# Linear attention plus routed MLP on one core: one-pass norm, K weights by row blocks, another warm-up, tile 3 transposed by DMA

## The chip, the cores and the metric

The kernel runs on one core of one Trainium2 chip. The metric is device time in microseconds (us) of one execution. TensorE (PE in the profile, PEld for its weight loads) does the matmuls and some transposes, VectorE (DVE) and ScalarE (ACT) the elementwise work, GpSimd (POOL) small work on columns and masks, SyncE (SP) issues most of the transfers. Each engine works through its own queue in order; semaphores tie the queues together.

## The reference

```python
def _layernorm(x, axis=-1, eps=1e-5):
    m = jnp.mean(x, axis=axis, keepdims=True)
    v = jnp.var(x, axis=axis, keepdims=True)
    return (x - m) / jnp.sqrt(v + eps)

def _A_ref(x, wqkv, wo):                     # H = 32 heads of 20
    q, k, v = split_heads(x @ wqkv)
    phi = lambda t: jnp.where(t > 0, t + 1, jnp.exp(t)) + 1e-6
    pq, pk = phi(q), phi(k)
    kv = jnp.einsum("bhsd,bhse->bhde", pk, v)
    z = jnp.einsum("bhsd->bhd", pk)
    num = jnp.einsum("bhqd,bhde->bhqe", pq, kv)
    den = jnp.einsum("bhqd,bhd->bhq", pq, z)[..., None] + 1e-6
    return merge_heads(num / den) @ wo

def _B_ref(x, w_r, w_gate, w_up, w_down):    # the C = 8 rows with the largest x @ w_r
    r = x @ w_r
    idx = jnp.argsort(-r, axis=-1)[:, :C]
    y = (_silu(x_sel @ w_gate) * (x_sel @ w_up)) @ w_down * _sigmoid(r_sel)
    return x + scatter_add(zero, idx, y)

xn = _layernorm(x)                           # x: (1, 2048, 640), bf16
return x + _A_ref(xn, A_wqkv, A_wo) + _B_ref(xn, B_w_r, B_w_gate, B_w_up, B_w_down)
```

Both branches read the same normalised rows. Everything is bf16 in memory; the intermediate size of the routed MLP is 1536.

## The kernel before, in words

The 2048 rows are 16 tiles of 128 rows (`T`), the 640 columns are 5 blocks of 128 (`KC`). `XX[:, t, 1, :]` holds tile t of x, `XX[:, t, 0, :]` the normalised tile, `xnT` the normalised rows transposed.

Every instruction is written out by hand in the order in which its engine takes it (`manual_schedule`), so that the order of the statements is the order of each engine's queue.

The kernel has a first pass over the 16 tiles and then work on weights, queries and outputs.

For each tile the first pass does the following.

- *Norm.* `ln_a` and `ln_b` (L159, L162) take the statistics of each half of the columns on DVE, `ln_g` (L165) joins them to mean and variance in `MV`, which are bf16 values kept in the upper halves of f32 words. `ln_s` (L198, L199) adds eps on DVE and raises to the power 0.5 on POOL. `ln_c` (L204 on ACT, L206 on DVE) writes mean minus x to a buffer `c`. `ln_xn` (L211, L213) takes the reciprocal of the root and multiplies `c` by it into `XX[:, t, 0, :]`. Tiles 1 and 5 get their statistics from ACT (`ln_act`, L173 to L177) and their root from POOL (`ln_msq`, `ln_var`, L186 to L193).
- *Transposing.* Tiles 0 to 3 are transposed by PE (`tr_pe`, L220) in five blocks, and copied out of PSUM by ACT in two pieces (L224). Tiles 4 to 15 are transposed by a DMA from SP (`tr_dma`, L229).
- *K.* `K(t)` (L251) multiplies the transposed tile by the K weights, in two halves of 320 columns; the second half has one more column, the router's weights `w_r`. `PHe` and `PHr` (L267, L270) take exp and relu on ACT, `PHb` (L286) joins them on DVE to `pk`.
- *G.* `G(t)` (L291, L296) adds the tile's product of normalised rows and `pk` to PSUM, where it stays until tile 15. `ones(t)` (L302, POOL) sets one column of the normalised tile to 1 first.

From tile 4 on a loop runs `K(t)`, then on DVE `PHb(t - 1)` and the norm of tiles up to t + 4, then `G(t - 1)`. The tiles before that are written out one by one (L380 to L454), and that is the part that the change reorders. There PE's order is K(2), tile 3's transposes, G(0), K(3), G(1), G(2), K(4).

The start, ahead of that: SP issues the loads of x tiles 0 to 2, the first half of the K weights, x tile 3, the second half in five pieces, and the other tiles. The router's column gets into the K weights by a transpose on PE (L138) and a copy on ACT (L141). PE does matmuls on zeros ahead of and behind that transpose: `warm4` (L122, f32, 512 columns) and `warm` (L127, bf16). A DMA transposes a block of zeros into the last columns of `xnT` (L379), which are written again later.

Behind the first pass PE goes on with the queries (L502), the small products of `G` with the V and output weights, the routed MLP, and the output tiles (L755), which DVE adds to x (L768) and SP stores.

Of the kernel before, what the change touches and what calls it, by code (L numbers as in the profile page):

```python
# [38 lines left out]
def kernel(  # L39
# [27 lines left out]
    def st(shape, dt, name, tag=None):  # L67
# [6 lines left out]
    wk = st([P, KC * (D + 1)], BF16, "wk", "wkM")  # L74
# [14 lines left out]
    halfc = st([P, 1], BF16, "halfc")  # L89
    epsb = st([P, 1], BF16, "epsb")  # L90
# [8 lines left out]
    wkh = [wk[:, 0 : KC * HW].rearrange("p (k c) -> p k c", k=KC),  # L99
           wk[:, KC * HW : KC * (D + 1)].rearrange("p (k c) -> p k c", k=KC)]  # L100
# [11 lines left out]
    ld(sp, XX[:, 1, 1, :], x_v[:, 1, :])  # L112
    ld(sp, XX[:, 2, 1, :], x_v[:, 2, :])
    ld(sp, wkh[0], wqkv_v[:, :, D : D + HW])
    ld(sp, XX[:, 3, 1, :], x_v[:, 3, :])


    zero32 = zero[:].bitcast(F32)

    def warm4(n):  # L120
        for _ in range(n):
            pe.matmul(PS[:, 7, :], lhsT=zero32[:, 0:P],  # L122
                      rhs=zero32[:, 0:256].unsqueeze(1).to_broadcast([P, 2, 256]), start=True, stop=True)

    def warm(n, w=512):
        for _ in range(n):
            pe.matmul(PS[:, 7, 0:w], lhsT=zero[:, 0:P], rhs=zero[:, 0:w], start=True, stop=True)  # L127
# [9 lines left out]
    warm4(1)  # L137
    pe.transpose(PS[:, 3, :].bitcast(BF16)[:, 0:KC], wr[:], ident[0:KC, 0:KC])  # L138
    warm4(1)
    warm(1)  # L140
    act.copy(wkh[1][:, :, HW], PS[:, 3, :].bitcast(BF16)[:, 0:KC])  # L141
    for kc in range(KC):
        ld(sp, wkh[1][:, kc, 0:HW], wqkv_v[:, kc, D + HW : 2 * D])
# [43 lines left out]

    def ln_var(t):
        pool.tensor_tensor(out=MV[:, t, 1:2], in0=sm[:, t, 1:2], in1=msq[:, 0:1], op=ALU.subtract)
        t2 = tmp.tile([P, 1], BF16, tag="t2", name="t2", bufs=4)  # L190
# [4 lines left out]
    def ln_s(t):
        t2 = tmp.tile([P, 1], BF16, tag="t2", name="t2", bufs=4)
        ss[t] = tmp.tile([P, 1], BF16, tag="s", name="s", bufs=4)
        dve.tensor_scalar(out=t2[:], in0=MV[:, t, 1:2], scalar1=EPS_BF16, scalar2=None, op0=ALU.add)  # L198
        pool.tensor_tensor(out=ss[t][:], in0=t2[:], in1=halfc[:], op=ALU.pow)  # L199

    def ln_c(t, eng):
        cs[t] = tmp.tile([P, D], BF16, tag="c", name="c", bufs=3)
        if eng is act:
            act.activation(cs[t][:], XX[:, t, 1, :], AF.Identity, bias=MVf[:, t, 0:1], scale=-1.0)  # L204
        else:
            dve.tensor_scalar(out=cs[t][:], in0=XX[:, t, 1, :], scalar1=MVf[:, t, 0:1], scalar2=-1.0,  # L206
                              op0=ALU.subtract, op1=ALU.mult)

    def ln_xn(t, parts=((0, D),)):
        c = cs[t]  # L210
        dve.reciprocal(SR[:, t : t + 1], ss[t][:])  # L211
        for a, b in parts:
            dve.tensor_scalar(out=XX[:, t, 0, a:b], in0=c[:, a:b], scalar1=SR[:, t : t + 1], scalar2=-1.0,  # L213
                              op0=ALU.mult, op1=ALU.mult)
# [32 lines left out]
    def K(t, hs=(0, 1), b=6):  # L247
        for h in hs:
            w = HW + h
            for kc in range(KC):  # L250
                pe.matmul(  # L251
                    PS[:, b + h, off(t, h) : off(t, h) + w],
                    lhsT=xnT[:, kc, t * P : (t + 1) * P],
                    rhs=wkh[h][:, kc, 0:w],
                    start=(kc == 0),
                    stop=(kc == KC - 1),
                )
# [121 lines left out]
    sp.dma_start_transpose(xnT[:, 0:4, S - P : S], zero[:])  # L379
# [567 lines left out]
```

## Time and profile before

| | us |
|---|---|
| median of 3 runs (range) | 108.45 (108.4 to 109.05) |
| the profiled execution, its own time | 108.45 |
| its span, first to last instruction | 106.7 |
| PE busy | 101.7 (95%) |
| DVE busy | 84.3 (79%) |
| ACT busy | 74.8 (70%) |
| POOL busy | 27.8 (26%) |

The span is what the profile shows; 1.75 us of the execution lie around it. A line of the profile begins with the start in us and the duration in us, or, in the tables of groups, ends with the busy time in us and the mean of one instruction in ns. L numbers are lines of the kernel before. Matmuls are pipelined: a row's duration holds the way through the array, so that the next one starts before it ends.

### The profile page before, as it was taken

To read this page: it belongs to the slowest core of one execution; us is meant where nothing else is said; L and a number is where in the kernel's file an instruction comes from. 1 tells how busy PE (TensorE), PEld (TensorE's weight loads), DVE (VectorE), ACT (ScalarE), POOL (GpSimd) and SP (SyncE) were. 2 spreads that over 40 slices of the span, in tenths; PEclk is the share of its full clock that TensorE was granted. 3 is DMA by queue.
4 is the path that set the end of the run, shared out by engine and by line. 5 is a ranking of instruction groups with operands and counts; after the bars stand their busy time and mean duration, and the time that the engine had idled before them with its cause. 6 is when DMAs were issued, how large, how long until landed. Compare 5 with 4: busy or idle time off the path is not lost.

```text
span 106.7 us, 2600 instructions
## 1 busy us (share of the span) xinstructions
PE 101.7 (95%) x923; PEld 62.6 (59%) x923; DVE 84.3 (79%) x207; ACT 74.8 (70%) x163; POOL 27.8 (26%) x79
## 2 busy tenths in 40 slices
PE   5979999999999999999999999999999999999990
PEld 1245656666666666667556545655656677777760
DVE  1789997999998999974898996729598696888870
ACT  4649996888877777888497999997688499200000
POOL 7437235456222222000000593500006200000410
PEclk9999999999999999999999999999999999999999
DMA  2999961435566875889998999901560224796344
GB/s 75 272 276 336 339 82 38 81 74 77 112 141 135 118 138 123 175 219 381 234 399 274 352 339 386 311 26 31 170 237 0 63 95 126 177 364 227 123 126 123
DMA packets 23247, 19.68 MB, mean 184 GB/s; under 512 B 10818, under 2 KB 21698, under 8 KB 23234
## 3 DMA queue, kind: packets, MB, share of 16 engines
q1 hardware_dynamic: 22712, 19.45, 65.5%
q8 instruction: 7, 0.11, 0.4%
q0 software_dynamic: 288, 0.01, 0.4%
q10 hardware_dynamic: 234, 0.06, 0.2%
q14 instruction: 6, 0.05, 0.2%
HBM read 13.80 MB, written 3.65 MB: 164 GB/s over the span
## 4 chain that ended last, share of the span: by engine, by line
PE 84%; DVE 7%; POOL 2%; issue 2%; ACT 1%; DVEq 0%; POOLq 0%
PE PS L502 21%; PE PS L755 19%; PE PS L251 15%; PE PS L291 15%; PE PS L296 3%; PE PS L122 2%; PE PS L678 2%; PE PS L715 2%; DVE XX L213 1%; DVE pk L286 1%; POOL s L199 1%; DVE stats L162 1%; PE PS L566 1%; PE PS L737 1%; PE PS L310 1%
## 5 line engine op out<-in xcount | busy, mean ns | idle before, releaser
L251 PE MATMUL PS<-wk,xnT 128*128 128x320 bf16 (+1 forms) x160 | 24.7, 300 | 0.6 <-ACT xnT L224 0.4
L291 PE MATMUL PS<-pk,XX 128*128 128x512 bf16 x80 | 23.2, 378 | 0.1
L502 PE MATMUL PS<-xnT,wq 128*128 128x512 bf16 x100 | 23.0, 380 | 0.0
L755 PE MATMUL PS<-Mb,pqT 128*128 128x320 bf16 (+2 forms) x165 | 22.1, 295 | 0.0
L251 PEld LDWEIGHTS <-xnT 128*128 128x128 bf16 x160 | 15.4, 98 | 7.4 <-ACT xnT L224 0.9
L755 PEld LDWEIGHTS <-pqT 128*128 128x128 bf16 x165 | 15.8, 97 | 6.4 <-issue 0.2
L267 ACT ACTIVATE ek<-PS 128x320 bf16<-128x320 f32 x32 | 14.3, 446 | 5.2 <-PE PS L251 5.2
L502 PEld LDWEIGHTS <-wq 128*128 128x128 bf16 x100 | 11.3, 118 | 9.0
L557 DVE SCALAR_TENSOR_TENSOR pqT<-qe,qr 128x512 bf16<-128x512 bf16 x20 | 13.5, 683 | 2.0 <-ACT qr L509 1.7
L768 DVE TENSOR_TENSOR o<-PS,XX 128x640 bf16<-128x640 f32 x15 | 12.2, 820 | 3.6 <-PE PS L755 2.8
L508 ACT ACTIVATE qe<-PS 128x512 bf16<-128x512 f32 x20 | 12.2, 609 | 3.8 <-PE PS L502 3.3
L270 ACT ACTIVATE rk<-PS 128x320 bf16<-128x320 f32 x32 | 14.4, 449 | 0.0
L199 POOL TENSOR_TENSOR s<-t,halfc 128x1 bf16<-128x1 bf16 x14 | 8.6, 617 | 21.7 <-DVE t L198 21.7
L296 PE MATMUL PS<-pk,XX 128*128 128x128 bf16 x64 | 14.0, 219 | 0.0
L286 DVE SCALAR_TENSOR_TENSOR pk<-ek,rk 128x640 bf16<-128x640 bf16 x16 | 13.0, 815 | 0.9 <-ACT rk L270 0.7
L291 PEld LDWEIGHTS <-XX 128*128 128x128 bf16 x80 | 7.7, 98 | 8.1
L509 ACT ACTIVATE qr<-PS 128x512 bf16<-128x512 f32 x20 | 12.1, 607 | 0.0
L204 ACT ACTIVATE c<-XX,MVf 128x640 bf16<-128x640 bf16 x10 | 8.4, 839 | 1.7 <-DVE MVf L165 1.6
L241 ACT ACTIVATE XX<-XX,MR,SR 128x640 bf16<-128x640 bf16 x11 | 9.4, 914 | 0.0
L159 DVE BATCH_NORM_STATS2 stats<-XX 128x6 f32<-128x320 bf16 x14 | 6.8, 486 | 1.9 <-DMA XX<-in_A_x_dram 1.9
L213 DVE TENSOR_SCALAR XX<-c,SR 128x640 bf16<-128x640 bf16 (+2 forms) x17 | 6.3, 377 | 1.3
L296 PEld LDWEIGHTS <-XX 128*128 128x128 bf16 x64 | 6.2, 97 | 1.3 <-issue 0.4
(125 smaller groups left out, 104.7 us busy)
## 6 DMA issues: line engine op xcount, KB each, us to landing
out_dram<-o SPq DMA_DIRECT2D x15, 160.0 KB, 2.3
wg<-in_B_w_gate_dram SPq DMA_DIRECT2D x5, 384.0 KB, 8.3
wu<-in_B_w_up_dram SPq DMA_DIRECT2D x5, 384.0 KB, 5.9
wd<-in_B_w_down_dram SPq DMA_DIRECT2D x1, 1920.0 KB, 10.7
XX<-in_A_x_dram SPq DMA_DIRECT2D x2, 640.0 KB, 7.1
wv<-in_A_wqkv_dram SPq DMA_DIRECT2D x5, 160.0 KB, 2.9
wq<-in_A_wqkv_dram SPq DMA_DIRECT2D x1, 800.0 KB, 5.4
hi_d<-XX SPq DMA_DIRECT2D x1, 800.0 KB, 4.5
```

What stands on the lines that cost most here:

```text
L251: pe.matmul(PS[:, b + h, off(t, h) : off(t, h) + w], lhsT=xnT[:, kc, t * P : (t + 1) * P], rhs=wkh[h][:, kc, 0:w], start=(kc == 0), stop=( ...
L267: act.activation(phis[t][0][:, h * HW : (h + 1) * HW], phi_src(t, h, b), AF.Exp)
L270: act.activation(phis[t][1][:, h * HW : (h + 1) * HW], phi_src(t, h, b), AF.Relu)
L286: dve.scalar_tensor_tensor(out=pk[:, t, :], in0=ek[:], scalar=1.0, in1=rk[:], op0=ALU.min, op1=ALU.add)
L291: pe.matmul(PS[:, a, :], lhsT=lhsT, rhs=pk[:, t, 0:512], start=(t == 0), stop=(t == T - 1),)
L296: pe.matmul(PS[:, 5, a * P : (a + 1) * P], lhsT=lhsT, rhs=pk[:, t, 512:D], start=(t == 0 and a == 0), stop=(t == T - 1), skip_group_check= ...
L502: pe.matmul(PS[:, bank, :], lhsT=by5(wq[:, kc, :])[:, m, :], rhs=xnT[:, kc, tb * TBLK : (tb + 1) * TBLK], start=(kc == 0), stop=(kc == KC ...
L508: act.activation(e, PS[:, bank, :], AF.Exp)
L509: act.activation(r, PS[:, bank, :], AF.Relu)
L557: dve.scalar_tensor_tensor(out=pqT[:, m, tb * TBLK : (tb + 1) * TBLK], in0=e, scalar=1.0, in1=r, op0=ALU.min, op1=ALU.add,)
L755: pe.matmul(PS[:, b_, 0 : c1 - c0], lhsT=pqT[:, kc, t * P : (t + 1) * P], rhs=Mb[:, kc, c0:c1], start=(kc == 0), stop=(kc == KC - 1))
L768: dve.tensor_tensor(out=ot[:].rearrange("p (h c) -> p h c", h=2), in0=PS[:, b : b + 2, 0:HW], in1=XX[:, t, 1, :].rearrange("p (h c) -> p h ...
```

## The change

- **Norm in one pass.** `ln_s`, `ln_c` and the variants for tiles 1 and 5 go. `ln_r` has ACT take Ln of variance plus eps and then Exp of -0.5 times that, which is the reciprocal root, into `SR`. `ln_xn` reads x and does (x - mean) * `SR` in one DVE instruction. The statistics of tiles 1 and 5 are taken on DVE like the others. The bf16 roundings between the steps fall away.
- **K weights in row blocks.** `wk` becomes one tile of five row blocks with a pitch of 656 columns (`WS`), loaded by five DMAs of 128 rows by 640 columns right behind x tile 1. The buffer `Mb`, which takes its place later, gets the same pitch.
- **Loads.** x tiles 2 to 11 follow the K weights; tiles 12 to 15 and the copies of the mask `bm2` are issued in the loop, at tile 5. The DMA that transposes zeros follows tiles 8 to 11.
- **Warm-up from constants.** `warm4` multiplies a constant that the program's preamble sets, instead of the memset tile. Three calls stand ahead of the router's transpose, one behind it; `warm` goes.
- **First tiles reordered.** K(0) goes block by block through both halves, tile 1's transposes stand between its fourth and fifth block, tile 2's between the third and fourth block of K(1)'s second half; the second PSUM copies of tiles 1 and 2 go to DVE. ACT's queue begins with the router's copy, Ln and Exp of tile 0, the first copy of tile 0, Ln and Exp of tile 1, the second copy of tile 0.
- **Tile 3** is transposed by DMA; PE's order is then K(2), G(0), K(3), G(1), G(2), K(4).

```diff
-    wk = st([P, KC * (D + 1)], BF16, "wk", "wkM")
+    wk = st([P, KC, WS], BF16, "wk", "wkM")
...
     ld(sp, XX[:, 1, 1, :], x_v[:, 1, :])
+    for kc in range(KC):
+        ld(sp, wk[:, kc, 0:D], wqkv_v[:, kc, D : 2 * D])
     ld(sp, XX[:, 2, 1, :], x_v[:, 2, :])
-    ld(sp, wkh[0], wqkv_v[:, :, D : D + HW])
     ld(sp, XX[:, 3, 1, :], x_v[:, 3, :])
+    ld(sp, XX[:, 4:6, 1, :], x_v[:, 4:6, :])
+    ld(sp, XX[:, 6:8, 1, :], x_v[:, 6:8, :])
+    ld(sp, XX[:, 8:12, 1, :], x_v[:, 8:12, :])
+    sp.dma_start_transpose(xnT[:, 0:4, S - P : S], zero[:])
...
-            pe.matmul(PS[:, 7, :], lhsT=zero32[:, 0:P],
-                      rhs=zero32[:, 0:256].unsqueeze(1).to_broadcast([P, 2, 256]), start=True, stop=True)
+            pe.matmul(PS[:, 7, :], lhsT=nc.const_aps.tensor(0.0, (P, P), F32),
+                      rhs=nc.const_aps.tensor(0.0, (P, 512), F32), start=True, stop=True)
...
-    warm4(1)
+    warm4(3)
     pe.transpose(PS[:, 3, :].bitcast(BF16)[:, 0:KC], wr[:], ident[0:KC, 0:KC])
     warm4(1)
-    warm(1)
-    act.copy(wkh[1][:, :, HW], PS[:, 3, :].bitcast(BF16)[:, 0:KC])
-    for kc in range(KC):
-        ld(sp, wkh[1][:, kc, 0:HW], wqkv_v[:, kc, D + HW : 2 * D])
+    act.copy(wk[:, :, D], PS[:, 3, :].bitcast(BF16)[:, 0:KC])
...
+    def ln_r(t):
+        act.activation(lnv[:, t : t + 1], MV[:, t, 1:2], AF.Ln, bias=eps5[:])
+        act.activation(SR[:, t : t + 1], lnv[:, t : t + 1], AF.Exp, scale=-0.5)
...
     def ln_xn(t, parts=((0, D),)):
-        c = cs[t]
-        dve.reciprocal(SR[:, t : t + 1], ss[t][:])
         for a, b in parts:
-            dve.tensor_scalar(out=XX[:, t, 0, a:b], in0=c[:, a:b], scalar1=SR[:, t : t + 1], scalar2=-1.0,
-                              op0=ALU.mult, op1=ALU.mult)
+            dve.tensor_scalar(out=XX[:, t, 0, a:b], in0=XX[:, t, 1, a:b], scalar1=MVf[:, t, 0:1],
+                              scalar2=SR[:, t : t + 1], op0=ALU.subtract, op1=ALU.mult)
...
+    consts_e()
     ln_a(0)
     ln_b(0)
     ln_g(0)
-    ln_s(0)
-    ln_msq(1)
-    ln_c(0, dve)
-    ln_c(1, dve)
+    ln_r(0)
+    ln_a(1)
     ln_xn(0, ((0, 3 * P), (3 * P, D)))
-    tr_pe(0, 0, act, act)
-    ln_var(1)
-    ln_a(2)
+    tr_pe(0, 0, act, act, (0,))
+    ln_b(1)
+    ln_g(1)
+    ln_r(1)
+    tr_pe(0, 0, act, act, (1,))
+    ones(0)
     ln_xn(1)
-    ln_b(2)
+    for kc in range(KC):
+        for h in range(2):
+            K_mm(0, h, kc, 6)
+        if kc == 3:
+            ln_a(2)
+            ln_b(2)
+            tr_pe(1, 2, act, dve)
+            ones(1)
     ln_g(2)
...
+    ln_xn(3)
+    tr_dma(3)
+    ones(3)
+    K(2)
     PHb(0)
...
```

163 lines of the change are left out of this document (47 added, 116 removed).

## The prediction

> **What bounds the kernel now.** The page first, for the span and the engines.
>
> ```profile
> span 106.7 us, 2600 instructions
> PE 101.7 (95%) x923; PEld 62.6 (59%) x923; DVE 84.3 (79%) x207; ACT 74.8 (70%) x163; POOL 27.8 (26%) x79
> GB/s 75 272 276 336 339 82 38 81 74 77 112 141 135 118 138 123 175 219 381 234 399 274 352 339 386 311 26 31 170 237 0 63 95 126 177 364 227 123 126 123
> ```
>
> TensorE (PE) is busy for 95% of the span, which is only an average. The stretches of 6 us say where it is not (columns: stretch, its length, then PE, PEld, DVE, ACT, POOL busy, clock, DMA share, GB/s).
>
> ```profile
> 14.00:20.00 6.00, 5.85 (x43) 3.48 (x42) 5.19 (x14) 5.09 (x15) 2.59 (x7) 1.00 0.35 67
> 20.00:26.00 6.00, 6.00 (x45) 3.73 (x44) 5.58 (x18) 4.94 (x12) 3.17 (x11) 1.00 0.37 57
> 92.00:98.00 6.00, 6.00 (x46) 4.29 (x45) 5.62 (x8) 0.00 (x0) 0.00 (x0) 1.00 0.88 296
> ```
>
> All 13 stretches from 20 to 98 us have PE busy 6.00 of 6.00. So the kernel has two parts: a start of some 15 us in which engines wait for each other, and then a stream of matmuls without a gap. The chain that ended last shows the seam.
>
> ```profile
> 3.46 0.17 ACT wk L141
> 13.15 0.62 POOL s L199
> 14.01 0.39 DVE XX L213
> 14.39 0.74 DVE pk L286
> 15.18 0.38 PE PS L291
> 17.94 1.37 PE PS L251 x10
> 20.62 1.37 PE PS L251 x10
> ```
>
> Until 14.39 the chain runs over VectorE (DVE), GpSimd (POOL) and ScalarE (ACT); from 15.18, the first matmul of G(1), it stays on PE. The matmuls from G(1) on are the same in both kernels. **So the time changes by what G(1)'s start changes, if PE stays fed afterwards.** What the change takes from DVE and ACT after 15.18 is worth nothing: not the ten 0.84 us passes of `ln_c` on ACT, nor the additions, reciprocals and POOL powers of tiles 6 to 15. PE hides them, and would have to run dry before they counted. The K weights' new row pitch has no gain either: the last two rows give ten K matmuls in 1.37 us, 137 ns each for 320 or 321 columns, already under the old pitch, and 2.67 us from one tile to the next.
>
> **The start, row by row.** PE and what hangs on it:
>
> ```profile
> 0.82 0.57 ACTq L104 DMA_DIRECT2D wr<-in_B_w_r_dram  x1
> 1.23 2.07 PE L122 MATMUL PS<-zero 128*128 128x512 f32 x2 [1.23 <-DVE MVf L109]
> 3.24 0.18 PE L138 MATMUL PS<-ident,wr 5*128 5x5 bf16 x1
> 3.35 2.03 PE L122 MATMUL PS<-zero 128*128 128x512 f32 x2
> 3.46 0.18 ACT L141 COPY wk<-PS 128x5 bf16<-128x5 bf16 x1 [1.39 <-PE PS L138]
> 4.07 0.21 DVE L165 BATCH_NORM_AGGREGATE MVf<-stats 128x2 bf16<-128x12 f32 x1
> 5.22 0.38 PE L127 MATMUL PS<-zero 128*128 128x512 bf16 x1
> 5.44 0.51 DVE L213 TENSOR_SCALAR XX<-c,SR 128x384 bf16<-128x384 bf16 x2
> 5.82 0.48 PE L220 MATMUL PS<-ident,XX 128*128 128x128 bf16 x5 [0.22 <-DVE XX L213]
> 6.19 0.75 ACT L224 COPY xnT<-PS 128x384 bf16<-128x384 bf16 x2 [0.80 <-PE PS L220]
> ```
>
> A warm-up call (an fp32 matmul, two records) holds PE from 1.23 to 3.24 and from 3.35 to 5.22: 2.01 and 1.87 us, 1.94 on average. Between them stands the router's 5x5 transpose, and ACT's copy of it (3.46) ahead of all its other work.
>
> *Warm-up.* Now three calls stand ahead of that transpose and one behind it. The constant needs no memset of DVE, so I start PE at 0.84, by the other engines' first work at 0.82. The calls start at 0.84, 2.78 and 4.72. What a call costs at a faster clock no row shows: 1.94 is one end, half of it (0.97) the other. The five transposes at 5.82 take 0.48 us with a wait inside, against 0.22 us for one alone, so PE is at its full rate there, 4.6 us after it began. I let the full rate begin at 5.2, where the second call ended. The third call then ends at 5.9, the transpose at 6.1, the fourth call at 6.9. If the full rate begins with the third call, the three are done at 5.7; if no call is faster, at 6.7, and the fourth at 8.6.
>
> [...]
>
> *One-pass norm.* Prices of its parts:
>
> ```profile
> 4.31 0.16 DVE L198 TENSOR_SCALAR t<-MVf 128x1 bf16<-128x1 bf16 x1
> 4.56 0.65 POOL L199 TENSOR_TENSOR s<-t,halfc 128x1 bf16<-128x1 bf16 x1 [1.44 <-DVE t L198]
> 5.24 0.16 DVE L211 RECIPROCAL SR<-s 128x1 f32<-128x1 bf16 x1 [0.16 <-POOL s L199]
> 64.85 0.20 ACT L630 ACTIVATE ge<-r 1x8 f32<-1x8 f32 x1
> 65.08 0.21 ACT L631 ACTIVATE gl<-ge 1x8 f32<-1x8 f32 x1
> L213 DVE TENSOR_SCALAR XX<-c,SR 128x640 bf16<-128x640 bf16 x15 | 5.8, 387 | 1.3
> L238 DVE TENSOR_SCALAR XX<-XX,SR,MR 128x640 bf16<-128x640 bf16 x5 | 2.0, 442 | 0.0
> L159 DVE BATCH_NORM_STATS2 stats<-XX 128x6 f32<-128x320 bf16 x14 | 6.8, 486 | 1.9 <-DMA XX<-in_A_x_dram 1.9
> L732 DVE COPY hT<-PS 128x384 bf16<-128x384 bf16 x1 | 0.4, 358 | 0.0
> L267 ACT ACTIVATE ek<-PS 128x320 bf16<-128x320 f32 x32 | 14.3, 446 | 5.2 <-PE PS L251 5.2
> ```
>
> From the aggregate's end (4.28) to the normalising pass (5.44) the old way took 1.16 us. Ln and Exp, dependent and tiny, cost 0.23 us each by L630 and L631: 0.5 to 0.55 with the two hand-overs, so 0.6 less per tile. The pass itself has two column operands like L238: 0.39 to 0.44 us, taken as 0.39. DVE loses `ln_c` (as long as the pass) and gains the statistics of tiles 1 and 5 (two at 0.49 and a 0.21 aggregate each), which ACT did, and the second copies of tiles 1 and 2 out of PSUM: two blocks of 128 columns, 0.33 us by L732, which took 0.36 for three. POOL, rid of the powers, has the time for the masks that it now makes before tile 0's column of ones.
>
> But ACT works in order, and the router's copy, which waits for PE's third call, is ahead of tile 0's Ln. Free, tile 0 would be normalised at 4.85. Behind the copy (6.12) Ln starts at 6.2, the pass at 6.7 instead of 5.44, the transposes at 7.05 instead of 5.82. **The gain of 0.6 becomes a loss of 1.2.** In the same way tile 1's Ln stands behind the first copy of tile 0's transposes (0.49 us), and the second copy behind that Ln and Exp; PE's last K(0) matmuls and tile 1's transposes wait for both.
>
> *K weights in row blocks* are taken at nothing. SP issues a transfer every 0.46 us, so x tile 2 goes out at about 4.0 instead of 1.7. Ahead of it are two tiles and five blocks, 1.15 MB; at 276 GB/s, the third slice of the page, they are through at about 6.0 and tile 2 is there by 7.0, and its statistics come at 8.7. The last block, there by 6.3, is needed at 9.5. If the loads came 2 us later they would show.
>
> *Tile 3 by DMA* takes five transposes off PE (0.28 us) and two copies off ACT, and puts a landing ahead of K(3).
>
> ```profile
> 7.85 1.99 SPq L379 DMA_TRANSPOSE xnT<-zero  x1
> xnT<-zero SPq DMA_TRANSPOSE x1, 7.6
> xnT<-XX SPq DMA_TRANSPOSE x12, 2.7
> L229 SPq DMA_TRANSPOSE xnT<-XX x12: 1200/1207/1654, 14.4 to 43.2; - x12
> DMA to landing us min/median/max: 2.6/2.7/3.2
> ```
>
> A tile takes 2.7 us from issue to landing. The transpose of zeros, issued behind the bulk loads, landed at 15.45; the new kernel moves 0.64 MB of them to tile 5's turn, 2 us at 336 GB/s, so it lands at about 13.4. SP then waits for tile 3's pass; behind stand only tile 4's and 5's transposes, the last load and the mask copies, needed later. [...]
>
> **The sum.** I laid out each engine's queue in order with these durations (successive DVE and ACT passes start 0.08 to 0.13 us before the earlier one's end; K(3) and the rest in PE's order). Laid over the old queues, this puts G(1) at 15.02, where the trace has 15.18; I use differences of the two layouts. Starts, old to new: first transposes 5.75 to 7.05 (+1.30); tile 1's 7.34 to 9.05 (+0.41 more); tile 2's 9.36 to 11.05 (-0.02); G(0) 12.03 to 13.45 (-0.27, tile 3's transposes gone); tile 3's pass is at 12.3, its DMA issued at 12.73 lands at 15.43, and K(3), ready at 14.75, waits 0.72; the old wait of G(1) for `pk` (0.33) is gone. G(1) starts at 16.84. **+1.8 us.**
>
> Afterwards a tile takes 2.67 us of PE, at most 2.3 of DVE (0.74 for `pk`, two 0.49, 0.21, 0.39) and 2.3 of ACT (four passes of 0.45, Ln and Exp), and tile 4's transpose lands at 18.2, ahead of K(4) at 19.4: no new wait. The profiled execution took 108.45 us, 1.75 around its span, and equals the median: 108.45 + 1.8 = 110.3.
>
> **Rivals.**
> 1. *No call gets faster before the fourth ends.* The router's copy comes at 6.9, PE takes the first transposes at 8.63, and G(1) comes at 18.4: +3.4, 111.9. For it: both measured calls cost nearly the same; against it: the full rate by 5.82.
> 2. *The full rate begins with the third call, and the DMA lands in time*, in 2.0 us instead of 2.7: G(1) at 16.12, +1.1, 109.6. For it: PE starts 0.4 earlier than before; against it: no landing of the twelve was under 2.6. [...]
> 3. *Not slower: the calls cost half from the start.* Then the copy is done before tile 0's aggregate, the first transposes come at 5.2, Ln and Exp give their 0.6, and with tile 3 landing in time G(1) is at 14.5: -0.5, 107.9. It decides where three calls end before 4.2, that is at 1.1 us each; 2.01 and 1.87 speak against it. With the landing behind the zeros' transpose it is 16.4 all the same.
> 4. *The change doesn't act as said*: PE bound before G(1) too, the ACT queue reordered by the build. The chain over POOL and DVE is against the first, the order of the built program against the second.
>
> **How the numbers follow.** Forecast (109.8 to 111.1, with the landing at 2.6 to 3.2 us) 0.5; rival 1 0.2; rival 2 0.15; rival 3 and 4, or a shorter start than I see, 0.15, half of it under 107.4. The range goes from 108.7, leaving out most of the last, to 111.9. One per cent, 1.1 us, is about what a measurement of this kernel tells from no change: slower by over 1% 0.76 (forecast, rival 1 and two fifths of rival 2), within 0.16, faster 0.08.
>
> **What would show it.** Right: the router's copy on ACT after 5.9; the first pass on XX near 6.7; the first transposes near 7; an idle PE ahead of K(3), ended by the DMA into xnT; then PE 6.00 of 6.00. Wrong: the first pass before 5.4, PE's calls under 1.2 us each, or gaps on PE after 20 us.

## The result, and the profile after

| | before | after |
|---|---|---|
| median, us (range) | 108.53 (108.4 to 109.05) | 111.72 (111.29 to 112.14) |
| the profiled execution | 108.45 | 112.14 |
| its span | 106.7 | 110.4 |

The changed kernel is slower: ratio 1.0285, 95% interval 1.0238 to 1.0333. Some executions of the kernels below stand more than 1.5% above the fastest of the same kernel; the ratios leave those out, the medians keep them.

The page of the changed kernel first, span and engines (busy us, share of the span, instructions).

```profile
span 110.4 us, 2537 instructions
PE 103.4 (94%) x911; PEld 63.2 (57%) x921; DVE 81.2 (74%) x180; ACT 69.4 (63%) x171; POOL 17.4 (16%) x55
```

The engines that the change wanted to relieve are relieved (DVE 84.3 to 81.2, ACT 74.8 to 69.4, POOL 27.8 to 17.4), and the kernel is 3 us longer. PE, with two more warm-up calls, is busy for 1.7 us more in a span that is 3.7 us longer, so waits have been added. Two of the stretches of 6 us shown for before, and the two behind them (line numbers are from here on those of the kernel that is profiled; columns: stretch, length, PE, PEld, DVE, ACT, POOL busy, clock, DMA share, GB/s):

```profile
14.00:20.00 6.00, 5.44 (x37) 3.07 (x37) 5.90 (x16) 4.42 (x16) 1.06 (x5) 1.00 0.36 73
20.00:26.00 6.00, 5.95 (x44) 3.84 (x43) 4.89 (x13) 3.66 (x12) 1.85 (x7) 1.00 0.57 68
26.00:32.00 6.00, 4.83 (x34) 2.87 (x33) 4.97 (x12) 3.66 (x12) 0.10 (x1) 1.00 0.94 189
32.00:38.00 6.00, 5.68 (x41) 3.67 (x42) 3.37 (x8) 3.66 (x12) 0.30 (x3) 1.00 0.55 118
```

Before, no stretch from 20 to 98 us had PE below 6.00. Now PE is short of work between 26 and 32, where the DMA share is 0.94. The chain that ended last has both places (start, duration, what):

```profile
0.84 5.46 PE PS L122 x6
6.41 1.06 PE PS L122 x2
...
13.46 2.58 DMA xnT<-XX
16.08 1.54 PE PS L201 x10
...
20.22 1.36 PE PS L201 x10
...
27.60 4.67 DMA xnT<-XX
```

The chain of before had K(4) at 17.94 where this one has it at 20.22: **the start is 2.28 us later.** Then two transposing DMAs stand in the chain, tile 3's (2.58 us) ahead of K(3) and tile 8's (4.67 us) ahead of K(8), where before there was no DMA at all. The rows of the start, put together from the timelines of PE, ACT and DVE (start, duration, engine, line, operation, idle time before it and what ended that):

```profile
6.24 0.17 PE L133 MATMUL PS<-ident,wr 5*128 5x5 bf16 x1
6.34 1.13 PE L122 MATMUL PS<-const-float32-0.0 128*128 128x512 f32 x2
6.45 0.18 ACT L135 COPY wk<-PS 128x5 bf16<-128x5 bf16 x1 [4.36 <-PE PS L133]
6.51 0.30 ACT L160 ACTIVATE lnv<-MVf,eps 128x1 f32<-128x1 bf16 x1
7.07 0.64 DVE L165 TENSOR_SCALAR XX<-XX,MVf,SR 128x384 bf16<-128x384 bf16 x2 [2.45 <-ACT SR L161]
7.51 0.54 PE L172 MATMUL PS<-ident,XX 128*128 128x128 bf16 x5
```

DVE stands for 2.45 us with tile 0's statistics done, because ACT's Ln waits behind the router's copy, and that behind three warm-up calls. When the pass is through its first part, PE still has the fourth call (6.34 to 7.47). And the rows of SP and PE around tile 8, with K(8) of the kernel before as the last row:

```profile
24.93 0.58 SPq L102 DMA_DIRECT2D XX<-in_A_x_dram  x1
25.60 1.90 SPq L102 DMA_DIRECT2D bm<-bm  x3
27.60 1.23 SPq L181 DMA_TRANSPOSE xnT<-XX  x1
32.31 1.54 PE L201 MATMUL PS<-wk,xnT 128*128 128x320 bf16 x10 [1.43 <-DMA xnT<-XX]
28.53 1.54 PE L251 MATMUL PS<-wk,xnT 128*128 128x320 bf16 x10
```

SP issues the 640 KB load of tiles 12 to 15 and three mask copies at tile 5's turn. Tile 8's transpose goes out behind them, at 27.60, and lands behind the load's data, 4.67 us later where the median of the transposes is 2.7. K(8) waits 1.43 us; before, it didn't wait. 2.28 + 1.43 = 3.71, and the two profiled executions differ by 3.69: the account closes for these two, of which the one after is the longest of its four. What follows tests it.

### The profile page after: what moved, and what is told of

It is laid out like the page before. It is cut to its first block, busy times and chain, and to the rows that moved or that the text cites. A ratio compares the mean times of both kernels' runs of the same rounds, so it can differ in the third digit from the quotient of the medians.

```text
span 110.4 us, 2537 instructions
## 1 busy us (share of the span) xinstructions
PE 103.4 (94%) x911; PEld 63.2 (57%) x921; DVE 81.2 (74%) x180; ACT 69.4 (63%) x171; POOL 17.4 (16%) x55
## 4 chain that ended last, share of the span: by engine, by line
PE 83%; DMA 7%; ACT 4%; issue 1%; DVE 1%; DVEq 0%
PE PS L439 20%; PE PS L692 19%; PE PS L201 16%; PE PS L246 12%; DMA xnT<-XX 7%; PE PS L122 6%; PE PS L251 3%; PE PS L615 1%; PE PS L652 1%; ACT ek L222 1%; ACT xnT L176 1%; PE PS L503 1%; ACT rk L225 1%; PE PS L674 1%; PE PS L265 1%
## 5 line engine op out<-in xcount | busy, mean ns | idle before, releaser
L246 PE MATMUL PS<-pk,XX 128*128 128x512 bf16 x75 | 22.4, 379 | 0.1
L222 ACT ACTIVATE ek<-PS 128x320 bf16<-128x320 f32 x32 | 14.0, 437 | 10.7 <-PE PS L201 10.7
L225 ACT ACTIVATE rk<-PS 128x320 bf16<-128x320 f32 x32 | 13.9, 434 | 0.0
L246 PEld LDWEIGHTS <-XX 128*128 128x128 bf16 x80 | 7.7, 98 | 8.1
L165 DVE TENSOR_SCALAR XX<-XX,MVf,SR 128x640 bf16<-128x640 bf16 (+2 forms) x17 | 7.3, 434 | 3.9 <-ACT SR L161 3.9
L151 DVE BATCH_NORM_STATS2 stats<-XX 128x6 f32<-128x320 bf16 x16 | 7.3, 458 | 1.9 <-DMA XX<-in_A_x_dram 1.9
L257 POOL MEMSET XX<- 128x1 bf16 x16 | 1.8, 115 | 41.0 <-DMA xnT<-XX 27.6
L154 DVE BATCH_NORM_STATS2 stats<-XX 128x6 f32<-128x320 bf16 x16 | 7.7, 481 | 0.0
L122 PE MATMUL PS<-const-float32-0.0 128*128 128x512 f32 x8 | 6.6, 973 | 0.8 <-PEq L868 0.8
```

Source lines behind the costliest of these rows:

```text
L122: pe.matmul(PS[:, 7, :], lhsT=nc.const_aps.tensor(0.0, (P, P), F32), rhs=nc.const_aps.tensor(0.0, (P, 512), F32), start=True, stop=True)
L222: act.activation(phis[t][0][:, h * HW : (h + 1) * HW], phi_src(t, h, b), AF.Exp)
L225: act.activation(phis[t][1][:, h * HW : (h + 1) * HW], phi_src(t, h, b), AF.Relu)
L246: pe.matmul(PS[:, a, :], lhsT=lhsT, rhs=pk[:, t, 0:512], start=(t == 0), stop=(t == T - 1),)
```

## The experiments

One table for all of them; times in us, places from PE's rows in the profiled execution. "First transposes" are tile 0's on PE, K(4) and K(15) the first matmul of that tile's K product.

| kernel | median | ratio to before, 95% | profiled | first transposes | K(4) | K(15) |
|---|---|---|---|---|---|---|
| before | 108.53 | | 108.45 | 5.82 | 17.78 | 47.25 |
| after | 111.72 | 1.024 to 1.033 | 112.14 | 7.51 | 20.06 | 50.98 |
| e1 warm-up as before | 110.39 | 1.007 to 1.015 | 111.34 | 5.27 | 19.35 | 50.19 |
| e2 masks late | 111.01 | 1.015 to 1.026 | 111.20 | 6.63 | 19.35 | 49.48 |
| e3 tile 3 on PE | 110.23 | 1.011 to 1.023 | 109.75 | 6.56 | 19.07 | 48.54 |
| e4 copy behind | 110.74 | 1.016 to 1.025 | 109.70 | 6.11 | 19.02 | 48.55 |
| e5 load early | 110.92 | 1.019 to 1.026 | 110.92 | 6.57 | 20.09 | 49.41 |
| e6 warm-up and x tile 2 | 110.77 | 1.016 to 1.021 | 110.75 | 5.26 | 18.47 | 49.57 |
| e7 norm alone | 109.84 | 1.010 to 1.014 | 109.76 | 5.52 | 19.04 | 48.51 |
| e8 warm-up alone | 111.06 | 1.016 to 1.030 | 111.06 | 7.33 | 19.70 | 49.82 |
| e9b norm by GpSimd's power | 108.26 | 0.993 to 0.996 | 108.33 | 5.65 | 17.67 | 47.10 |
| e10 four undone | 109.74 | 1.006 to 1.013 | 109.58 | 5.26 | 18.63 | 47.95 |
| e11 five undone | 109.30 | 1.003 to 1.009 | 108.70 | 5.32 | 17.87 | 47.19 |
| e12 power on GpSimd | 111.25 | 1.015 to 1.025 | 111.26 | 5.59 | 19.13 | 49.17 |

The profiled execution is one of several and can lie at the edge of its kernel's range (e1 and the changed kernel high, e3, e4 and e11 low), so places are compared with its own time. In the kernels that keep the three calls ahead of the router's transpose (the changed one, e2 to e5, e8) the calls alone differ by 1.2 us from profile to profile (last section). With 3 or 4 runs each, the medians of these kernels therefore price a single edit no closer than about 1 us, an estimate from that spread, and the account goes by places.

### The warm-up

e1 is the changed kernel with the calls as before:

```diff
-    warm4(3)
+    warm4(1)
...
+    pe.matmul(PS[:, 7, :], lhsT=zero[:, 0:P], rhs=zero[:], start=True, stop=True)
```

> The changed kernel with the warm-up as before (one call ahead of the router's transpose, one call and one bf16 matmul behind it). Theory A (PE held by warm-up calls is the late start): router's copy near 3.4, PE free for the first transposes at 5.5 instead of 7.5, first matmul of G(1) 1.0 to 2.0 us earlier than 17.45 (the less if tile 3's DMA then waits behind the zeros' transpose, which lands at 14.1), time 109.7 to 110.8. Theory B (the order of ACT's queue is the late start, whatever PE does): under 0.5 us, 111.2 to 111.8.

It gives back 1.3 of the 3.2 us by the medians and 1.9 by the ratios; its seven executions range from 109.13 to 111.34, and the profile is of the longest. The start of its timelines of PE and DVE, and K(8):

```profile
5.27 0.65 PE L173 MATMUL PS<-ident,XX 128*128 128x128 bf16 x5
8.18 0.84 PE L202 MATMUL PS<-wk,xnT 128*128 128x320 bf16 x5 [0.29 <-DMA wk<-in_A_wqkv_dram]
8.67 0.50 DVE L152 BATCH_NORM_STATS2 stats<-XX 128x6 f32<-128x320 bf16 x1 [1.47 <-DMA XX<-in_A_x_dram]
31.53 1.54 PE L202 MATMUL PS<-wk,xnT 128*128 128x320 bf16 x10 [1.35 <-DMA xnT<-XX]
```

Tile 0's transposes come 2.24 us earlier than in the changed kernel, G(1) and K(4) only 0.7, less than the 1.0 to 2.0 that was expected. In between, a K-weight block is 0.29 late and x tile 2 1.47: the new order of the loads, hidden behind the late start in the changed kernel, is the next limit. K(8) waits nearly as long as in the changed kernel (1.35 us), which no part of the start touches.

e6 goes on from e1 and loads x tile 2 ahead of the last three blocks:

```diff
-    for kc in range(KC):
+    for kc in range(2):
         ld(sp, wk[:, kc, 0:D], wqkv_v[:, kc, D : 2 * D])
     ld(sp, XX[:, 2, 1, :], x_v[:, 2, :])
+    for kc in range(2, KC):
+        ld(sp, wk[:, kc, 0:D], wqkv_v[:, kc, D : 2 * D])
```

> The changed kernel with the warm-up as before and x tile 2's load ahead of the last three K row blocks. In the run with the old warm-up alone, tile 2's statistics waited 1.5 us for its load (landing 8.64, issued 4.11, behind five blocks). Theory (the load order is the next limit, hidden in the changed kernel behind the warm-up): tile 2 lands near 7, its statistics start 7.3 to 7.7 instead of 8.67, first matmul of G(1) 0.5 to 1.0 us earlier than 16.9, time 109.3 to 109.9; the last K block lands later, near 8.4, and takes up to 0.5 us of it back. Rival (bandwidth, not order): tile 2 early makes K(0) wait as long, time as with the old warm-up alone, 110.4.

K(4) comes 0.88 us earlier than in e1, about as expected, but the time is not the 109.3 to 109.9 of the theory: it is no better than e1's. K(8) has taken 0.26 of the 0.88, by the timeline of PE:

```profile
30.90 1.54 PE L204 MATMUL PS<-wk,xnT 128*128 128x320 bf16 x10 [1.61 <-DMA xnT<-XX]
```

The wait grew from 1.35 to 1.61: what comes earlier at K(4) partly waits longer at K(8), since tile 8's transpose still stands behind the load. K(15) keeps 0.62 of the 0.88. Why the median shows none of it is open; e1's profile is of its longest execution, so the two profiles don't compare like their medians.

e4 leaves the warm-up and puts the router's copy behind tile 0's Ln and Exp:

```diff
     pe.transpose(PS[:, 3, :].bitcast(BF16)[:, 0:KC], wr[:], ident[0:KC, 0:KC])
     warm4(1)
-    act.copy(wk[:, :, D], PS[:, 3, :].bitcast(BF16)[:, 0:KC])
...
     ln_r(0)
+    act.copy(wk[:, :, D], PS[:, 3, :].bitcast(BF16)[:, 0:KC])
```

> The changed kernel with the router's copy behind tile 0's Ln and Exp in ACT's queue. Theory A: tile 0 is normalised at 4.9 instead of 7.07, but PE's fourth call still ends at 7.47, so the first transposes stay at 7.5 and the time within 0.3 us of 111.7. Theory B (ACT's order): the first transposes come near 5.2, G(1) 1 to 2 us earlier, time 109.7 to 110.7.

PE's rows:

```profile
0.85 4.26 PE L122 MATMUL PS<-const-float32-0.0 128*128 128x512 f32 x6 [0.85 <-PEq L868]
6.11 0.44 PE L171 MATMUL PS<-ident,XX 128*128 128x128 bf16 x5
```

The pass is early now (4.86), but the transposes still stand behind the fourth call, that is behind PE's own queue, as theory A had it. They begin 1.00 us after the end of the three calls, against 1.20 to 1.21 in the changed kernel, e2, e3 and e5: that is all the copy costs while the calls stay. Copy and calls are two locks on one door. The same six records took 5.46 us in the changed kernel and 4.26 here, which no edit of e4 touches. Of the 2.4 us by which this profile is shorter, K(4) has 1.04, and K(8), which hardly waits here, about 1.4 (below); so the 1.0 us of the medians, more than theory A allowed, is not shown to be the copy's.

e8 puts the changed warm-up alone into the kernel before:

```diff
-                      rhs=zero32[:, 0:256].unsqueeze(1).to_broadcast([P, 2, 256]), start=True, stop=True)
+                      rhs=nc.const_aps.tensor(0.0, (P, 512), F32), start=True, stop=True)
...
-    warm4(1)
+    warm4(3)
...
-    warm(1)
```

> The kernel before with only the warm-up of the changed one (three calls from constants ahead of the router's transpose, one behind). Theory: the router's copy on ScalarE near 6 to 6.5 instead of 3.46, the first transposes on PE at 6.1 to 8.0 by the moment at which the full rate comes, G(1) 0.8 to 2.2 us later than 15.18, time 109.4 to 110.8. Rival (the calls are hidden behind the norm of tile 0): under 0.4 us, time 108.4 to 109.0.

It costs 2.3% there, by itself. Rows of ACT, DVE and PE:

```profile
5.31 0.18 ACT L140 COPY wk<-PS 128x5 bf16<-128x5 bf16 x1 [3.24 <-PE PS L138]
6.46 0.39 DVE L205 TENSOR_SCALAR c<-XX,MVf 128x640 bf16<-128x640 bf16 x1 [1.76 <-ACT MVf L173]
7.33 0.48 PE L219 MATMUL PS<-ident,XX 128*128 128x128 bf16 x5 [1.00 <-DVE XX L212]
```

There it isn't PE that is late (it waits 1.00 for the pass) but ACT: the router's copy holds tile 1's statistics, and they hold DVE, which has tile 0's pass behind tile 1's `c`. G(1) is 1.92 us later, within the theory's 0.8 to 2.2; the time is a little above its 109.4 to 110.8, since K(11) comes 3.31 us after K(10) instead of 2.67, at the end of a wait for its transpose.

### The late load and tile 3's DMA

e2 moves the mask copies to tile 12, e5 moves the load of tiles 12 to 15 to the start as well, e3 has tile 3 transposed by PE again:

```diff
         if t == 5:
             ld(sp, XX[:, 12:16, 1, :], x_v[:, 12:16, :])
-            bm2_copies(sp, (1, 2, 3))
...
         if t == 12:
+            bm2_copies(sp, (1, 2, 3))
```

> The changed kernel with the three mask copies issued at tile 12 instead of tile 5; the load of tiles 12 to 15 stays at tile 5. If SP's issue time (1.9 us of mask copies between tile 8's pass, done at 26.3, and its transpose, issued at 27.6) makes K(8) wait 1.43 us: the transpose goes out at 26.3, K(8) waits 0 to 0.2, time 110.3 to 110.6. If the transfer itself is late because the load of 640 KB is ahead of it in the DMA queues (landing 4.67 instead of 2.6 us): issue is earlier, the landing still near 31.5 to 32.3, K(8) waits 0.7 to 1.4, time 111.0 to 111.7.

Rows of SP and PE:

```profile
24.22 0.57 SPq L102 DMA_DIRECT2D XX<-in_A_x_dram  x1
25.58 1.21 SPq L181 DMA_TRANSPOSE xnT<-XX  x1
30.78 1.54 PE L201 MATMUL PS<-wk,xnT 128*128 128x320 bf16 x10 [0.61 <-DMA xnT<-XX]
```

All of e2 from K(4) on stands 0.71 earlier than the changed kernel. Net of that the transpose is issued 1.3 us earlier, and lands 0.8 earlier (30.73, just behind the load, whose last part landed at 30.17): 5.15 us after its issue. So with SP's 1.90 us for the copies gone, the load ahead in the queues still sets the landing, and 0.61 of the wait is left, a result between the two that were expected.

```diff
+    ld(sp, XX[:, 12:16, 1, :], x_v[:, 12:16, :])
     sp.dma_start_transpose(xnT[:, 0:4, S - P : S], zero[:])
...
-        if t == 5:
-            ld(sp, XX[:, 12:16, 1, :], x_v[:, 12:16, :])
-            bm2_copies(sp, (1, 2, 3))
...
+            bm2_copies(sp, (1, 2, 3))
```

> The changed kernel with the load of tiles 12 to 15 at the start as before (ahead of the transpose of zeros) and the mask copies at tile 12. Theory (tile 8's transpose stands behind that load in the DMA queues, first in, first out): K(8) waits no more, tile 8 lands under 3.2 us after issue; but the zeros' transpose lands near 15.5 instead of 14.0, so tile 3's lands no earlier than 16.7, and K(3) waits longer where the start was fast. Time 110.3 to 111.0. Rival (transposes are late by themselves at that place): K(8) still waits over 0.5 us, time above 111.

PE's rows of K(3) and K(8):

```profile
16.11 1.54 PE L202 MATMUL PS<-wk,xnT 128*128 128x320 bf16 x10 [1.37 <-DMA xnT<-XX]
30.75 1.52 PE L202 MATMUL PS<-wk,xnT 128*128 128x320 bf16 x10
```

K(8) waits no more, as expected, and K(3) waits 1.37 instead of 0.41: the zeros' transpose, now behind all the loads, lands at 15.55, and tile 3's, behind it, at 16.07. Early or late, the 640 KB stand in front of a transposing DMA on which PE waits. Before, no DMA transpose was due by then.

```diff
-    tr_dma(3)
-    ones(3)
     K(2)
+    PHa(2, (0,))
+    tr_pe(3, 2, act, act)
+    ones(3)
...
-    PHa(2, (0,))
```

> The changed kernel with tile 3 transposed by PE and copied by ACT as before, behind K(2). Theory A: the wait of 0.4 to 0.6 us ahead of K(3) goes, five transposes (0.28 us) come back on PE ahead of G(0): G(1) 0 to 0.3 us earlier, time 111.4 to 111.8. Rival (the DMA of tile 3 is the main loss of the start, as it is the longest piece of the chain, 2.58 us): G(1) over 1 us earlier, time under 110.8.

Without the wait in front of K(3), K(4) comes at 19.07, against 19.35 in e2 whose first transposes are as early (6.56 and 6.63): tile 3's DMA costs 0.2 to 0.3 us net, less than its wait of 0.41, since PE and ACT get the transposes and copies back. The time and G(1), 0.98 us earlier, are near those of the rival, but not by its cause: the start is 0.95 earlier from the calls on, and K(8) waits almost nothing in this profile (29.88, where 27.07 + 2.67 = 29.74 was due).

So the size of K(8)'s wait is not settled by what is issued ahead. Six profiled kernels have the load at tile 5, and K(8) waits 1.43 (changed kernel), 1.35 (e1), 0.61 (e2), 0.14 (e3), 0.21 (e4) and 1.61 us (e6). The load landed 5.1 us after its issue in e3, 5.2 in e4, 5.3 in the changed kernel and 5.8 to 6.1 in e1, e2 and e6. Nor is that all. The trace counts sixteen completions for each of these transfers. In the changed kernel the load had all of its own by 30.25, the copies theirs by 30.94, and tile 8's transpose fourteen by 31.08; the last two came at 32.16 and 32.27. In e3 and e4 all sixteen followed the copies within 0.2 us. What makes the load quicker in some executions, and two parts of a transpose late in another, stays open. That the wait comes from the move of the load and the copies to tile 5 is shown by e5, where it is gone.

### The norm

e7 is the kernel before with the one-pass norm by Ln and Exp and the order that goes with it (statistics of tiles 1 and 5 on ACT as before; tile 0's Ln and Exp between the two halves of tile 1's statistics, tile 1's between tile 0's two PSUM copies; tile 3's statistics ahead of tile 1's exp and relu):

```diff
-    def ln_s(t):
...
+    def ln_r(t):
+        act.activation(lnv[:, t : t + 1], MV[:, t, 1:2], AF.Ln, bias=eps5[:])
+        act.activation(SR[:, t : t + 1], lnv[:, t : t + 1], AF.Exp, scale=-0.5)
...
-    ln_act(1)
+    ln_act1(1)
...
+    ln_r(0)
+    ln_act2(1)
```

> The kernel before with only the one-pass norm: Ln and Exp on ScalarE for all tiles, no pass to c, the statistics of tiles 1 and 5 still on ScalarE, the loads, warm-up, K weights and tile 3's transposes as before; tile 3's statistics stand ahead of tile 1's exp and relu so that its Ln isn't queued behind them. Theory (the norm is a gain of about 0.6 us a tile in the start, lost in the changed kernel to the late start): first pass near 5.1 instead of 5.44, tile 3's pass 0.5 to 1.0 us earlier than 11.46, G(1) 0.5 to 1.2 us earlier than 15.18, time 107.4 to 108.1. Rival (the norm itself is a loss, since Ln and Exp stand in ScalarE's queue): G(1) later than 15.18, time above 108.7.

Slower by 1.2%, with G(1) at 16.43 instead of 15.18, as the rival had it. Rows of ACT and DVE for tiles 3 and 4, with tile 3's pass of the kernel before as the last row:

```profile
10.43 0.81 ACT L207 COPY xnT<-PS 128x384 bf16<-128x384 bf16 x2
11.07 0.35 ACT L191 ACTIVATE lnv<-MVf,eps 128x1 f32<-128x1 bf16 x1
11.69 0.45 DVE L196 TENSOR_SCALAR XX<-XX,MVf,SR 128x640 bf16<-128x640 bf16 x1 [0.24 <-ACT SR L192]
14.45 0.45 DVE L196 TENSOR_SCALAR XX<-XX,MVf,SR 128x640 bf16<-128x640 bf16 x1 [0.92 <-ACT SR L192]
11.46 0.39 DVE L213 TENSOR_SCALAR XX<-c,SR 128x640 bf16<-128x640 bf16 x1
```

Tiles 0 and 2 are normalised 0.36 and 0.44 earlier than before (5.08, 8.66), tiles 3 and 4 later by 0.23 and 0.44: their variance is ready at 9.75 and 13.17, and Ln (11.07 and 13.81) comes behind exps, relus and two PSUM copies each time. From 4 to 17 us ACT is busy for 11.4 of 13.0 us here, DVE for 8.9, and the one-pass norm puts a round trip through ACT's queue.

e9b does the same pass, but lets GpSimd make the reciprocal root, where it made the root:

```diff
-    pool.memset(halfc[:], 0.5)
+    pool.memset(halfc[:], -0.5)
...
-        pool.tensor_tensor(out=ss[t][:], in0=t2[:], in1=halfc[:], op=ALU.pow)
+        pool.tensor_tensor(out=SR[:, t : t + 1], in0=t2[:], in1=halfc[:], op=ALU.pow)
...
-            dve.tensor_scalar(out=XX[:, t, 0, a:b], in0=c[:, a:b], scalar1=SR[:, t : t + 1], scalar2=-1.0,
-                              op0=ALU.mult, op1=ALU.mult)
+            dve.tensor_scalar(out=XX[:, t, 0, a:b], in0=XX[:, t, 1, a:b], scalar1=MVf[:, t, 0:1],
+                              scalar2=SR[:, t : t + 1], op0=ALU.subtract, op1=ALU.mult)
```

> The kernel before with the one-pass norm alone, but 1/sqrt(var + eps) made by one power of -0.5 on GpSimd, where the power of 0.5 stood, instead of ln and exp on ScalarE: the centring pass c (0.38) and the reciprocal (0.16) go from VectorE (and c of the later tiles from ScalarE), nothing is put on ScalarE's queue. If it was ScalarE's queue that made the one-pass norm alone slower: pass of tile 0 near 5.25 (was 5.44), tile 2 near 8.7 (9.10), tile 3 near 10.7 (11.46), G(1) 0.4 to 0.8 earlier than 15.18, time 107.7 to 108.2. Rival (the pass itself, with two column operands at 0.44 instead of 0.39 and nothing between the power and the pass, costs what it saves, or PE and ScalarE's exps set G(1) anyway): G(1) within 0.2 of 15.18 and 108.3 to 108.8.

108.26 against 108.67 for before on the same chip, ratio 0.9944 (0.9926 to 0.9962): the one version here that beats both kernels, if by less than 1%. The time is just above the theory's 107.7 to 108.2, and G(1) is 0.37 us earlier, just short of its 0.4 to 0.8. So it is where the root is made that cost e7 its time, not the pass. Rows of DVE and POOL show why it isn't more:

```profile
8.13 0.55 POOL L195 TENSOR_TENSOR SR<-t,halfc 128x1 f32<-128x1 bf16 x1 [1.40 <-DVE t L194]
9.97 0.82 DVE L272 SCALAR_TENSOR_TENSOR pk<-ek,rk 128x640 bf16<-128x640 bf16 x1
10.09 1.11 POOL L195 TENSOR_TENSOR SR<-t,halfc 128x1 f32<-128x1 bf16 x1 [0.27 <-DVE t L194]
11.24 0.45 DVE L199 TENSOR_SCALAR XX<-XX,MVf,SR 128x640 bf16<-128x640 bf16 x1 [0.44 <-POOL SR L195]
```

Tile 3's power, 0.55 to 0.58 us for tiles 0 to 2, took 1.11 when it began at 10.09, just behind the start of `PHb` (9.97). The pass came at 11.24 instead of the 10.7 of the expectation; and of the 0.37 that G(1) gained (14.81), K(4) kept 0.11, its weight loads waiting 0.43 for tile 4's transpose, which landed 3.57 us after its issue. Ahead of it the last load of x, the zeros' transpose and SP's mask copies landed at 16.2, 16.8 and by 17.2 (before: 14.9, 15.4 and by 15.8).

### Setting everything back at once

e10 is the changed kernel with four things set back: the warm-up (e1's lines), x tile 2's place (e6's), the load of tiles 12 to 15 with the masks at tile 12 (e5's), tile 3 on PE (e3's). Kept are norm, row blocks and order. The load stands ahead of the zeros' transpose:

```diff
     ld(sp, XX[:, 8:12, 1, :], x_v[:, 8:12, :])
+    ld(sp, XX[:, 12:16, 1, :], x_v[:, 12:16, :])
...
-    warm4(3)
+    warm4(1)
...
-    tr_dma(3)
+    tr_pe(3, 2, act, act)
```

> The changed kernel with four things set back: the warm-up as before, tile 2's load ahead of the last three k-weight blocks, the load of tiles 12 to 15 at the start with the mask copies at tile 12, tile 3 transposed on TensorE. Kept: the one-pass norm by ln and exp, the row blocks of the k weights, the order of the first six tiles. My account (start +2.27, of it the warm-up and tile 2's load about 1.4, tile 3's wait about 0.5; tile 8's wait 1.43): first transposes near 5.3, no wait in front of K(3) or K(8), G(1) between 15.2 and 15.9, time 108.5 to 109.3, within 1% of before. Rival (the norm through ScalarE's queue costs a time of its own in the new order as it did alone, +1.2): G(1) at 16.2 or later and 109.6 to 110.2.

109.74, so some 2 of the 3.2 us are back, but G(1), at 16.03, and K(4) are 0.85 later than before, and the time is above the 108.5 to 109.3 of the account. It is in the rival's range; whether for the rival's reason, the next runs tell. PE's rows, with tile 1's transposes of the kernel before as the last:

```profile
7.86 0.43 PE L205 MATMUL PS<-wk,xnT 128*128 128x320 bf16 x2 [0.66 <-DMA wk<-in_A_wqkv_dram]
8.13 0.44 PE L176 MATMUL PS<-ident,XX 128*128 128x128 bf16 x5
7.42 0.44 PE L220 MATMUL PS<-ident,XX 128*128 128x128 bf16 x5
```

PE stops for 0.66 us in the middle of K(0) for the fourth row block, and tile 1's transposes, ordered behind it, come at 8.13 instead of 7.42. Two runs tell the row blocks from ACT's queue. e11 goes back to the K weights' old loads and halves:

```diff
-    for kc in range(2):
-        ld(sp, wk[:, kc, 0:D], wqkv_v[:, kc, D : 2 * D])
     ld(sp, XX[:, 2, 1, :], x_v[:, 2, :])
-    for kc in range(2, KC):
-        ld(sp, wk[:, kc, 0:D], wqkv_v[:, kc, D : 2 * D])
+    ld(sp, wk[:, :, 0:HW], wqkv_v[:, :, D : D + HW])
     ld(sp, XX[:, 3, 1, :], x_v[:, 3, :])
+    for kc in range(KC):
+        ld(sp, wk[:, kc, HW:D], wqkv_v[:, kc, D + HW : 2 * D])
...
+    K(0, (0,))
+    ln_a(2)
+    ln_b(2)
+    tr_pe(1, 2, act, dve)
+    ones(1)
+    K(0, (1,))
```

> The kernel of the four things set back (109.74 us; K(4) at 18.63 where before has 17.78), and a fifth: the k weights again as one load of 320 columns and five loads of the rest, tile 0's K blocks again by halves with tile 1's transposes between. Theory L (what is left comes from the row blocks: 0.66 us wait for a k-weight block in front of tile 1's transposes, which stand at 8.13 against 7.42): no wait in K(0), tile 1's transposes at 7.2 to 7.5, K(4) at 17.9 to 18.1, 108.6 to 109.0 us. Theory A (what is left comes from Ln and Exp in ScalarE's queue, which make the copies and the statistics wait): tile 1's transposes earlier, but the passes of tiles 2 and 3 still at 9.7 and 11.5, K(4) at 18.4 or later, 109.4 to 109.8 us.

PE's rows of tile 1's transposes and K(4):

```profile
7.37 0.44 PE L175 MATMUL PS<-ident,XX 128*128 128x128 bf16 x5
17.87 1.53 PE L204 MATMUL PS<-wk,xnT 128*128 128x320 bf16 x10
```

Places as the theory of the row blocks has them; K(15), at 47.19, is level with before (47.25). This profile is of one of the shortest of ten executions; the median (109.3, runs from 108.65 to 111.67) is above the theory's 108.6 to 109.0, and the intervals of e10 and e11 overlap. So the row blocks' 0.76 us at K(4) rests on the places. e12 keeps the row blocks and takes the power on GpSimd instead of Ln and Exp:

```diff
-        act.activation(lnv[:, t : t + 1], MV[:, t, 1:2], AF.Ln, bias=eps5[:])
-        act.activation(SR[:, t : t + 1], lnv[:, t : t + 1], AF.Exp, scale=-0.5)
+        dve.tensor_scalar(out=t2[:], in0=MV[:, t, 1:2], scalar1=EPS_BF16, scalar2=None, op0=ALU.add)
+        pool.tensor_tensor(out=SR[:, t : t + 1], in0=t2[:], in1=halfc[:], op=ALU.pow)
```

> The kernel of the four things set back (109.74 us), with 1/sqrt by one power of -0.5 on GpSimd instead of ln and exp on ScalarE (the masks' first part moved on GpSimd behind tile 6's statistics); k weights in row blocks as in the changed kernel. Theory A (ScalarE's queue): passes of tiles 2 and 3 0.3 to 0.8 earlier, K(4) at 17.9 to 18.2, 108.7 to 109.1 us. Theory L (row blocks): the wait of 0.66 in K(0) stays, tile 1's transposes near 8.1, K(4) at 18.4 or later, 109.4 to 109.8 us.

Neither: 1.5 us slower than e10 by the medians, 1.1 by the ratios. Rows of DVE and POOL:

```profile
14.12 0.81 DVE L245 SCALAR_TENSOR_TENSOR pk<-ek,rk 128x640 bf16<-128x640 bf16 x1
14.28 1.05 POOL L165 TENSOR_TENSOR SR<-t,halfc 128x1 f32<-128x1 bf16 x1 [1.18 <-DVE t L164]
15.37 0.45 DVE L169 TENSOR_SCALAR XX<-XX,MVf,SR 128x640 bf16<-128x640 bf16 x1 [0.44 <-POOL SR L165]
```

In the new order the powers of tiles 4 to 6 begin right behind the start of `PHb` and take 1.05 us each, DVE waits for them, and the next `PHb` and tile 5's transpose come late (K(5) at 22.50, against 21.30 in e10). With this cost of its own, e12 can't tell what ACT's queue costs. e11 can: it keeps Ln and Exp on ACT, and its K(4) is within 0.1 us of before. ACT's queue is thus not what is left in e10; the norm by Ln and Exp does fit the new order, which keeps them ahead of the copies and exps. One remainder: the five kernels with the masks at tile 12 (e2, e5, e10, e11, e12) lose another 0.3 to 0.9 us behind K(15), against under 0.1 in all others (the table's "profiled" less K(15)). By PE's timelines 0.3 to 0.7 of it lies ahead of the first output matmul; the cause stays open.

## Why the prediction was right, and where it fell short

Direction and range held (111.72 in 108.7 to 111.9); the forecast, +1.8, was little more than half of the +3.2 between the medians, and its own interval, 109.8 to 111.1, was missed. That the range held is in part luck: its upper end, 111.9, is the first rival's time, and what filled it, the wait of K(8), stands in no rival. One of the signs that were to show the text wrong, gaps on PE after 20 us, came. By its own steps:

- **The frame held.** The later start and what PE starves of afterwards are the whole difference of the two profiles: 2.28 + 1.43 against 3.69.
- **Warm-up: right in its mechanism, short in size.** ACT's copy after 5.9 (6.45), the pass near 6.7 (7.07), the transposes near 7 (7.51): each 0.3 to 0.5 late. The calls ran at the slow rate longer than forecast (three done at 6.24, forecast 5.9), the fourth ended at 7.47 (forecast 6.9), and Ln took 0.30 instead of 0.23. The transposes so came 0.46 later than forecast; G(1)'s +1.8 became +2.27. In other executions the calls end earlier (last section), and e2, e3 and e5 have the transposes at 6.56 to 6.63. Half of 1.94 for a call at the faster rate, 0.97, was the author's estimate; e4's third call took 1.02.
- **One-pass norm: the 0.6 per tile is right for a free ACT and wrong in a queue.** Aggregate to pass was 0.83 us in e7 for tile 0 (1.16 before), but 1.94 for tile 3 (1.33 before). The layout had ACT's queue in it, so the sum isn't wrong by this; but the text prices the norm as a gain that only the router's copy spoils, and e7 shows it as a loss of its own. The pass took 0.44 to 0.45, the upper end, not the 0.39 that was taken.
- **K weights "taken at nothing"** came out so in the changed kernel, but only because the late start covered it: x tile 2 landed at 7.97 there, not 7.0, and with the cover gone it was 1.47 late (e1) and a block 0.66 (e10); K(4) is 0.76 earlier without the row blocks (e11 against e10). The price of the lost cover was not worked out, as it should have been.
- **Tile 3 by DMA: right.** 2.58 us from issue to landing (2.7), a wait of 0.41 in front of K(3) (0.72), PE's wait ended by the DMA into `xnT` as said.
- **The failed step: "behind stand only tile 4's and 5's transposes, the last load and the mask copies, needed later", and from it "no new wait".** The working checked tile 4's landing and stopped. The load is needed late, but tile 8's transpose stands behind it and the copies in SP's queue and in the DMA queues, and K(8) waited 1.43 us: a term sized at nothing. Without the copies 0.61 of it is left (e2), without both nothing (e5). How long the wait is differs from profile to profile, 0.14 to 1.61 us, for a reason that stays open.
- **The rivals.** The first (111.9) has the time and not the mechanism: the fourth call took 1.1 us, so the full rate came before it ended. The second had the DMA in 2.0 us; it took 2.58. The third, an earlier start, needed calls of 1.1 us from the beginning; the first three took 5.4.

## What to carry to other kernels

Follow a moved load to every later instruction of the same queue, not only to the data's own reader: a bulk load moved into a steady loop can delay the small transfers behind it (here tile 8's transpose, 4.67 us to its landing against a median of 2.7). A step costed at nothing because a later one hides it has a price as soon as the cover goes, and in a start-up phase each undone delay uncovers the next: the old warm-up brought tile 0's transposes forward by 2.24 us and K(4) by 0.71, and only five edits together gave back all of K(15)'s delay. Counting what an engine is relieved of says little; ask in which queue the new dependent step stands, and behind what.

## What the runs showed of the hardware

**When TensorE gets to its full rate varies from run to run.** The third of the fp32 calls took 1.91 us in the changed kernel (first row) and 1.02 in e4, though the first began at 0.84 and 0.85:

```profile
4.39 1.91 PE L122 MATMUL PS<-const-float32-0.0 128*128 128x512 f32 x2
4.08 1.02 PE L122 MATMUL PS<-const-float32-0.0 128*128 128x512 f32 x2
```

All six records of the three calls, first matmul at 0.83 to 0.85 us, took 5.46 us (after), 4.58 (e2), 4.53 (e5), 4.51 (e3), 4.34 (e8) and 4.26 (e4). The profile's clock column shows 1.00 from 4 to 8 us of the changed kernel, where a call took 1.91 us and the next 1.13, and doesn't tell the two rates apart. Before, only the first call stands in the chain, from 1.23 to 3.30, and all executions took 108.4 to 109.05; the changed kernel waits for the fourth. What sets the moment, no run shows.

**GpSimd's power took twice as long behind the start of `PHb`.** On one column it took 1.05 to 1.11 us where it began just behind the start of `PHb` on DVE, and 0.55 to 0.58 elsewhere (e9b, e12). In the kernel before, the power of tile 6, begun at 18.12, 0.17 us behind `PHb`, took 1.06, and that of tile 3, begun at 10.41, 0.12 us ahead of `PHb`, took 0.61. Why, no run shows.

**A transposing DMA issued behind a bulk load landed behind it.** From issue to landing it took 2.6 to 3.2 us in the kernel before (median 2.7). Behind 640 KB of the same queue it took 5.15 when issued 1.4 us after the load (e2), and 4.67 (after), 3.3 (e4) and 3.2 (e3) when issued 2.7 us after it; in all four it landed 0.6 to 2.0 us after the load had.
